# First head pair of an attention kernel: decays on 128 rows, a cumulative sum in two parts, identity products in PE's waits

## The chip, the cores and the metric

The kernel runs on one core of a Trainium2 chip. The metric is the device time of one execution in microseconds. A profiled execution lists for every instruction its engine, start and duration. The engines are PE (TensorE, the matrix engine; its weight loads are listed as PEld), DVE (VectorE), ACT (ScalarE), POOL (GpSimd) and SP (SyncE, which here only issues DMAs). Each takes its instructions in the order in which they stand in its queue.

## The reference

Attention with a forget gate, and two mixtures of experts behind it. Only the attention matters here:

```
scores = scale * np.matmul(q, k.transpose(0, 1, 3, 2))
log_f = np.log(np.clip(f, 0.0001, 1.0))
cum = np.cumsum(log_f, axis=-1)
decay = cum[:, :, :, None] - cum[:, :, None, :]
scores = np.where(causal, -1000000000.0, scores + decay)
scores = scores - np.max(scores, axis=-1, keepdims=True)
attn = np.exp(scores)
attn = attn / (np.sum(attn, axis=-1, keepdims=True) + 1e-09)
return np.matmul(attn, v).astype(np.float32)
...
x = _moe_ref(x=x, **moe_kwargs)
return _moe2_ref(x=x, **moe2_kwargs)
```

There are 2 batches of 8 heads, 576 positions and a head dimension of 64. A row's softmax does not change when a constant is added to the row, so only the column term of `decay`, minus `cum` of the key's position, is needed.

## The kernel before, in words

The attention works on eight pairs of heads (`B * NP`), one pair after the other. A pair has five steps: four blocks of 128 query rows (i = 0 to 3), each with the keys up to its diagonal, and a tail (i = 4) of the last 64 rows of both heads together. The loop at the end of the attention runs over all 40 steps `n`; in one turn it transposes the exponentials of step n - 2 (`emit_tp`), makes the scores of step n (`emit_s`) and, one turn later still, multiplies the transposed exponentials with v (`emit_av`). Steps 0 and 1 of pair 0 are made by `startup` ahead of the loop. The schedule is manual: each engine's queue has the order in which the code is written.

Scores need more precision than one pass of the matrix engine in its fast float type (F32R) gives. So k is split in a high part `kh` (a cast by DVE) and a low part `kl` (a subtraction by POOL). One tile `qa` holds the high part of q in one half of its rows and the low part in the other (a cast, then `q_low`, a subtraction on 64 rows by POOL or DVE). For every head a score block is three products that add up in one bank: `qa` with `kh` (L315), `qa` with `kl` (L316) and an identity with the causal mask (L317). DVE then adds the decay `bi` and takes the row's extreme in one instruction (an eviction, L323), ACT takes the exponential (L326). The key split of a pair is `split_k` (cast L290, subtractions L293), the q split `split_q` (cast L301, subtractions by the helper `sub`, L156).

For pairs 1 to 7 the decays come by DMA from `nbd`, a copy of minus eight times the cumulative sum in memory, spread to 128 partitions. Pair 0 cannot wait for that. It makes its decays on PE: `neg8[:, h:h + 1]` broadcast over 128 columns as the weights, 16 rows deep, times `cum` (L542), and ACT copies them to `bi` (L544). The cumulative sum itself is one scan on 16 partitions by DVE over 576 columns (L506), behind a clip (L503) and a logarithm by ACT (L504, with its table load). ACT loads the exponential's table ahead of the first exponential (L326).

While PE waits for the cumulative sum it does seven products of the identity with itself, 128 columns each (L510, `WARM`). They go to a bank that nobody reads. An ordinary float product is carried out as two passes, each with its own weight load, so seven products are 14 in the profile.

SP issues in this order: `f`, pair 0's k and q in two parts, pair 1's k and q, v of pair 0, two small tables (`dps`, `wgs`), `nbd`, pair 0's tail decays, then pair 2's k and q, pair 1's decays and v.

Of the kernel before, what the change touches and what calls it, by code (L numbers as in the profile page):

```python
# [40 lines left out]
NX = 5  # L41
LAG_TP, LAG_AV = 2, 3
AVS = {1: (0, 1), 3: (2, 3), 4: (4,)}
WARM = 7


@with_exitstack
def kernel(
# [180 lines left out]
    with ExitStack() as at:  # L229
# [9 lines left out]
        ps_a = pool(at, "ps_a", 1, space=PSUM)  # L239

        identb, neg8, maskd, maskt = [sm_p.tile(sh, dt, name=nm, bufs=1) for nm, sh, dt in (
            ("identb", [P, P], BF16), ("neg8", [B * H, B * H], F32), ("maskd", [P, P], BF16), ("maskt", [P, 64], BF16))]
        kls = [spl_p.tile([P, 2, S], F32R, tag=f"kl{i}", name=f"kl_{i}", bufs=1) for i in range(2)]
        state = {}

        def load_qk(p):
            raw = raw_p.tile([P, QKW], F32, tag="raw", name=f"qk_{p}")
            SY.dma_start(out=raw[:, QW:QKW], in_=qk[p, :, QW:QKW])
            SY.dma_start(out=raw[:, 0:QW], in_=qk[p, :, 0:QW])
            state[p] = dict(raw=raw)  # L250
# [51 lines left out]
            for h in range(2 if p > 1 else 1):  # L302
                q_low(p, h, G)

        def emit_s(p, i, between=lambda: None):
            st = state[p]
            qa, kh, kl, bi = st["qa"], st["kh"], st["kl"], st["bi"]
            if i < 4:
# [3 lines left out]
                for h in range(2):  # L312
                    ps = ps_s.tile([P, 512], F32, tag="ps", name=f"s_{p}_{i}_{h}")
                    q0 = TOPAD * h + i * P
                    T.matmul(out=ps[:, :n], lhsT=qa[:, q0:q0 + P], rhs=kh[:, h, :n], start=True, stop=False)  # L315
                    T.matmul(out=ps[:, :n], lhsT=qa[:, q0:q0 + P], rhs=kl[:, h, :n], start=False, stop=False)  # L316
                    T.matmul(out=ps[:, i * P:w], lhsT=identb, rhs=maskd, start=False, stop=True)  # L317
# [161 lines left out]
        def startup():  # L479
            ft = e_p.tile([B * H, S], F32, tag="e0", name="ft")  # L480
            SY.dma_start(out=ft, in_=f)
            first_loads()
            bi = bia_p.tile([P, 3, S], F32, tag="bias", name="bias_0")
            vt = raw_p.tile([P, 5, P], F32, tag="v", name="v_0")
            G.memset(neg8, 0.0)
# [5 lines left out]
            G.memset(ident, 0.0)  # L491
            G.affine_select(out=ident, in_=ident, compare_op=ALU.not_equal, fill=1.0, base=0,
                            pattern=[[-1, P]], channel_multiplier=1)
            one_s = e_p.tile([B * H, S], F32, tag="e0", name="one_s")
            V.memset(one_s, 1.0)
            for h in range(2):
                V.memset(kls[0][64 - 64 * h:128 - 64 * h, h, :].bitcast(F32), 0.0)
# [24 lines left out]
            def k_part(c0, c1):  # L522
                V.tensor_copy(out=kh[:, :, c0:c1], in_=rk[:, :, c0:c1])
                for h in range(2):
                    rows = slice(64 * h, 64 * h + 64)
                    G.tensor_tensor(out=kl[rows, h, c0:c1], in0=rk[rows, h, c0:c1],
                                    in1=kh[rows, h, c0:c1].bitcast(F32), op=ALU.subtract)

            def q_part(c0, c1):
                if c0 == 0:  # L530
                    A.copy(out=sq[:, :, c0:c1], in_=rq[:, :, c0:c1])
                else:
                    V.tensor_copy(out=sq[:, :, c0:c1], in_=rq[:, :, c0:c1])
                for h in range(2):
                    rows = slice(64 - 64 * h, 128 - 64 * h)
                    V.tensor_tensor(out=sq[rows, h, c0:c1], in0=rq[rows, h, c0:c1],
                                      in1=sq[rows, h, c0:c1].bitcast(F32), op=ALU.subtract)

            def bias_part(c0, c1):
                for h in range(2):  # L540
                    ps = ps_a.tile([P, 512], F32, tag=("rp", "avt")[h], name=f"b_{c0}_{h}")
                    T.matmul(out=ps[:, 0:c1 - c0], lhsT=neg8[:, h:h + 1].to_broadcast([B * H, P]),  # L542
                             rhs=cum[:, c0:c1], start=True, stop=True)
                    A.copy(out=bi[:, h, c0:c1], in_=ps[:, 0:c1 - c0])  # L544

            load_qk(1)
            SY.dma_start(out=vt, in_=v[0])
            SY.dma_start(out=dps, in_=dp)
            SY.dma_start(out=wgs, in_=wg)
            k_part(0, CUT)  # L550
            q_part(0, CUT)
            bias_part(0, P)
            emit_s(0, 0)
            k_part(CUT, S)
            bias_part(P, 2 * P)
            nb8 = e_p.tile([B * H, S], F32, tag="e0", name="nb8")
            V.tensor_scalar(out=nb8, in0=cum, scalar1=-8.0, scalar2=None, op0=ALU.mult)
# [4 lines left out]
            emit_s(0, 1)  # L562
            q_part(CUT, TOPAD)
            for h in range(2):
                G.memset(kls[1][64 - 64 * h:128 - 64 * h, h, :].bitcast(F32), 0.0)
            bias_part(2 * P, S)

        def patterns():
            G.memset(upper, 1.0)
# [21 lines left out]

        steps = [(p, i) for p in range(B * NP) for i in range(5)]
        at.enter_context(tc.manual_schedule())
        startup()
        for n in range(2, len(steps) + LAG_AV):
            if n == len(steps) + 1:
                early_product("p1")
            if 0 <= n - LAG_TP < len(steps):
                emit_tp(*steps[n - LAG_TP])
                if steps[n - LAG_TP][1] == 3:  # L600
                    emit_inv(steps[n - LAG_TP][0])
            if n == len(steps) + 1:
# [12 lines left out]
            if n < len(steps):  # L615
                p, i = steps[n]
                nx = p + 1 if p + 1 < B * NP else None
                if (p, i) == (0, 2):
                    split_k(1)
                    split_q(1)  # L620
                    patterns()
                if p and i == 1 and nx:
                    split_q(nx)
                if i == 4 and p + 2 < B * NP:
                    split_k(p + 2)
                if i == (1 if p else 3) and nx:
                    if p + 2 < B * NP:
                        load_qk(p + 2)
                    load_pair(nx)
# [789 lines left out]
```

## Time and profile before

| | us |
|---|---|
| median of 3 runs | 604.86 (603.96 to 605.48) |
| the profiled execution, its own time | 604.12 |
| its span, first to last instruction | 602.4 |
| PE busy | 589.4 (98%) |
| DVE, ACT, POOL busy | 322.7, 262.2, 331.2 |

A busy share is a mean over stages. The first 36 us are read here instruction by instruction; PE's busy time counts an instruction from its start to the end of its drain, so neighbours overlap. The time from one start to the next is PE's pace. Pair 0 runs from 0 to about 22.6 us, pair 1 from there to 35.28.

### The profile page before, as it was taken

What the parts mean: (1) busy time and instruction counts of PE and PEld (TensorE: products, weight loads), DVE (VectorE), ACT (ScalarE), POOL (GpSimd) and SP (SyncE); (2) the same over time, 40 slices, a digit from 0 to 9 for tenths busy, and PEclk for the clock granted to TensorE, in tenths of its full rate; (3) what the DMA queues carried; (4) which work ended last, traced back from release to release, by engine and by line L of the source; (5) the groups of instructions that cost most, each with busy time, mean ns of one, the idle gap of its engine ahead of it and who ended that gap; (6) DMA issues with size and microseconds to landing.
All of it is one profiled execution on the core that took longest, in us unless ns stands there. A gap on an engine that the chain in (4) does not pass through costs nothing. (4 is left out here: it accounts for less than half of the span.)

```text
span 602.4 us, 10714 instructions
## 1 busy us (share of the span) xinstructions
PE 589.4 (98%) x3981; PEld 491.9 (82%) x3981; DVE 322.7 (54%) x821; ACT 262.2 (44%) x665; POOL 331.2 (55%) x382
## 2 busy tenths in 40 slices
PE   8999999999999999999999999999999999999995
PEld 6788888998898898998998989989989775555674
DVE  6888877655454544544544535535436467311483
ACT  5678798674243343334334325315314222112481
POOL 4878989799278169159239329419614143322321
PEclk9999999999999999999999999999999999999999
DMA  6895730401112011011101201102255976999940
GB/s 210 265 319 166 264 108 23 140 27 55 63 70 71 1 67 40 35 26 48 67 1 70 71 1 70 71 1 71 70 210 226 357 277 223 411 419 423 382 156 24
DMA packets 19175, 84.32 MB, mean 140 GB/s; under 512 B 2965, under 2 KB 4001, under 8 KB 11953
## 3 DMA queue, kind: packets, MB, share of 16 engines
q1 hardware_dynamic: 16832, 73.19, 33.7%
q0 software_dynamic: 2288, 10.42, 4.4%
q8 instruction: 32, 0.52, 0.4%
q14 instruction: 23, 0.18, 0.1%
HBM read 79.57 MB, written 5.28 MB: 141 GB/s over the span
## 5 line engine op out<-in xcount | busy, mean ns | idle before, releaser
L872 PE MATMUL dn<-w2h,hh 128*128 128x512 f32 x288 | 114.4, 397 | 0.0
L874 PE MATMUL dn<-w2h,hl 128*128 128x512 f32 x288 | 112.4, 390 | 0.0
L873 PE MATMUL dn<-w2l,hh 128*128 128x512 f32 x288 | 112.2, 390 | 0.0
L884 DVE SCALAR_TENSOR_TENSOR acc<-dn,dps,acc 128x512 f32<-128x512 f32 (+1 forms) x64 | 47.4, 743 | 97.9 <-PE dn L874 97.7
L156 POOL TENSOR_TENSOR w2l<-rawd,w2h 128x512 fp32r<-128x512 f32 x32 | 40.5, 1296 | 94.5 <-ACT w2h L201 94.5
L220 PE MATMUL p<-xb_h,w 128*128 128x320 f32 x224 | 69.2, 309 | 0.0
L219 PE MATMUL p<-xb_l,w 128*128 128x320 f32 x224 | 69.2, 309 | 0.0
L218 PE MATMUL p<-xb_h,w 128*128 128x320 f32 x224 | 69.1, 309 | 0.0
L874 PEld LDWEIGHTS dn<-w2h,hl 128*128 128x128 f32 x288 | 54.0, 188 | 11.5
L872 PEld LDWEIGHTS dn<-w2h,hh 128*128 128x128 f32 x288 | 54.1, 188 | 11.3 <-issue 1.4
L873 PEld LDWEIGHTS dn<-w2l,hh 128*128 128x128 f32 x288 | 54.1, 188 | 9.9
L218 PE MATMUL p<-xa,w 128*128 128x256 f32 x218 | 61.3, 281 | 0.0
L220 PE MATMUL p<-xa,w 128*128 128x256 f32 x218 | 61.2, 281 | 0.0
L219 PE MATMUL p<-xa,w 128*128 128x256 f32 x218 | 61.2, 281 | 0.0
L201 ACT CAST w2h<-rawd 128x512 fp32r<-128x512 f32 x32 | 18.3, 621 | 84.8 <-PE dn L874 84.8
L156 POOL TENSOR_TENSOR hl<-m,hh 128x256 fp32r<-128x256 f32 (+1 forms) x32 | 25.8, 808 | 43.4 <-ACT hh L834 43.4
L828 DVE SCALAR_TENSOR_TENSOR hl<-p,hh 128x320 fp32r<-128x320 f32 (+1 forms) x62 | 28.5, 459 | 36.0 <-ACT hh L827 36.0
L156 POOL TENSOR_TENSOR w<-ws,w 128x512 fp32r<-128x512 f32 x32 | 40.7, 1297 | 3.4 <-ACT w L175 3.4
L219 PEld LDWEIGHTS p<-xb_l,w 128*128 128x128 f32 x224 | 42.0, 188 | 0.3
L218 PEld LDWEIGHTS p<-xb_h,w 128*128 128x128 f32 x224 | 42.1, 188 | 0.3
L220 PEld LDWEIGHTS p<-xb_h,w 128*128 128x128 f32 x224 | 42.1, 188 | 0.0
L218 PEld LDWEIGHTS p<-xa,w 128*128 128x128 f32 x218 | 41.3, 190 | 0.3
(292 smaller groups left out, 1333.8 us busy)
## 6 DMA issues: line engine op xcount, KB each, us to landing
wm<-in_m SPq DMA_DIRECT2D x32, 1024.0 KB, 10.1
rawu<-in_w SPq DMA_DIRECT2D x8, 1024.0 KB
rawd<-in_w SPq DMA_DIRECT2D x8, 1024.0 KB, 4.7
qk<-in_qk SPq DMA_DIRECT2D x7, 640.0 KB
qk<-in_qk SPq DMA_DIRECT2D x7, 576.0 KB
bias<-nbd SPq DMA_DIRECT2D x14, 288.0 KB, 6.9
v<-in_v SPq DMA_DIRECT2D x8, 320.0 KB, 5.3
bias<-nbd SPq DMA_DIRECT2D x16, 144.0 KB, 6.2
```

The source lines that it names most:

```text
L156: eng.tensor_tensor(out=out, in0=a, in1=b, op=ALU.subtract)
L201: A.copy(out=ws["d", u][0][:, c, :], in_=wr["d", u][:, c, :])
L218: T.matmul(out=ps, lhsT=wt[:, 0, a, i, :], rhs=xh[:, i, :], start=(i == 0), stop=False)
L219: T.matmul(out=ps, lhsT=wt[:, 0, a, i, :], rhs=xl[:, i, :], start=False, stop=False)
L220: T.matmul(out=ps, lhsT=wt[:, 1, a, i, :], rhs=xh[:, i, :], start=False, stop=(i == 1))
L828: V.scalar_tensor_tensor(out=hl[:, j, cs], in0=c, scalar=0.0, in1=hh[:, j, cs].bitcast(F32), op0=ALU.max, op1=ALU.subtract)
L872: T.matmul(out=ps, lhsT=hh[:, j, ks], rhs=wh[:, j, :], start=(j == 0), stop=False)
L873: T.matmul(out=ps, lhsT=hh[:, j, ks], rhs=wl[:, j, :], start=False, stop=False)
L874: T.matmul(out=ps, lhsT=hl[:, j, ks], rhs=wh[:, j, :], start=False, stop=(j == 3))
L884: V.scalar_tensor_tensor(out=a, in0=ps[:, c0:c1], scalar=pe, in1=a, op0=ALU.mult, op1=ALU.add)
```

## The change

Decay products. `neg8` and `cum` now have 128 rows. Rows 16 to 127 of both are zero there (a clear of `cum` on DVE, a wider `neg8` on POOL), and the product takes all 128 rows. The two halves of a decay (`bias_mm` on PE, `bias_copy` on ACT) are written apart, and the first two share a bank.

Cumulative sum. The scan is made over the first 256 columns, and later over the other 320 from the first one's last column on; the clear and the first decay of 128 columns stand between. `nb8` and the store to `nbd` come ahead of the first eviction.

Identity products. `fill(n)` puts n products of the identity with its first 64 columns into PE's queue, to a bank that nobody reads. There are 18, 3, 2, 5, 2 and 5 of them (`FILLS`) at six places, the last in the loop's first turn. The identity is the first thing that POOL makes.

Order of work. In the first two score blocks of pair 0 the products with `kl` come behind those with `kh` and the mask of both heads (`gaps`). The subtractions of q are cut in smaller pieces over DVE and POOL. The clears of `kl` all go to POOL. The exponential's table is loaded by a small exponential (`junk`) ahead of the bias copies. Pair 1's key split moves from behind step 2 to the end of `startup`, pair 2's from behind step 4 of pair 0 to behind step 0 of pair 1. SP issues pair 1's decays and v ahead of pair 2's k and q, and the two small tables last.

PE's queue at the start of the program, before: the decay products are `b_...`, the score blocks of pair 0 `s_<block>_<head>`, the transposes `tp_<block>_<head>`.

```order
L510 MATMUL warm<-ident 128x128 x7
L542 MATMUL b_0_207<-cum,neg_143 128x128
L542 MATMUL b_1_210<-cum,neg_143 128x128
L315 MATMUL s_0_0_213<-kh_192,qa_191 128x256
L316 MATMUL s_0_0_213<-kl_146,qa_191 128x256
L317 LDWEIGHTS identb
L317 MATMUL s_0_0_213<-maskd,identb 128x128
L315 MATMUL s_0_1_217<-kh_192,qa_191 128x256
L316 MATMUL s_0_1_217<-kl_146,qa_191 128x256
```

The same place now (`hot` is the bank of the identity products):

```order
L524 MATMUL hot_189<-ident 128x64 x18
L550 MATMUL b_0_213<-cum,neg_143 128x128
L550 MATMUL b_1_215<-cum,neg_143 128x128
L524 MATMUL hot_189<-ident 128x64 x3
L315 MATMUL s_0_0_236<-kh_191,qa_190 128x256
L318 LDWEIGHTS identb
L318 MATMUL s_0_0_236<-maskd,identb 128x128
L315 MATMUL s_0_1_239<-kh_191,qa_190 128x256
L318 LDWEIGHTS identb
L318 MATMUL s_0_1_239<-maskd,identb 128x128
L323 MATMUL s_0_0_236<-kl_146,qa_190 128x256
L550 MATMUL b_0_213<-cum,neg_143 128x128
```

More identity products stand ahead of the first decays, and three between these and the first scores; the product with `kl` has gone behind the second head's.

DVE's queue where pair 0 ends and pair 1 starts, before (`sn_t` are the evictions of pair 0's tail, `kh_399` is the key cast of pair 2, `qa_301` the low part of q of pair 1):

```order
L344 ISA sn_t,mn_t_388<-s_t_382,bias_157,mn_t_380 128x288
L344 ISA mn_t_388 128x1
L290 CAST kh_399<-qk_352 128x1152
L156 TENSOR_TENSOR qa_301<-qk_195,qa_301 64x640
L377 COPY et_3_1_418<-tp_3_1_413 128x512
L355 SCALAR_TENSOR_TENSOR rs_194<-sum_193 128x9
```

The same place now (`qa_306` is that low part, `kh_468` the key cast of pair 2):

```order
L349 ISA sn_t,mn_t_420<-s_t_414,bias_160,mn_t_412 128x288
L349 ISA mn_t_420 128x1
L156 TENSOR_TENSOR qa_306<-qk_157,qa_306 64x640
L382 COPY et_3_1_443<-tp_3_1_438 128x512
L360 SCALAR_TENSOR_TENSOR rs_193<-sum_192 128x9
L361 RECIPROCAL sum_192<-rs_193 128x9
L328 ISA sn_0_0_457,mn_0_0_458<-s_0_0_449,bias_271 128x128
L328 ISA mn_0_0_458 128x1
L328 ISA sn_0_1_462,mn_0_1_463<-s_0_1_453,bias_271 128x128
L328 ISA mn_0_1_463 128x1
L290 CAST kh_468<-qk_389 128x1152
```

The key cast of pair 2 has gone from ahead of pair 1's low part of q to behind the first two evictions of pair 1.

The diff, cut to its core:

```diff
-WARM = 7
+FILLS = (18, 3, 2, 5, 2, 5)
...
+                for h in range(2 if gaps else 0):
+                    gaps[h]()
+                    q0 = TOPAD * h + i * P
+                    T.matmul(out=pss[h][:, :n], lhsT=qa[:, q0:q0 + P], rhs=kl[:, h, :n], start=False, stop=True)
...
-            cum = e_p.tile([B * H, S], F32, tag="sneg", name="cum")
-            V.tensor_tensor_scan(out=cum, data0=one_s, data1=lf, initial=0.0, op0=ALU.mult, op1=ALU.add)
-
-            warm = ps_s.tile([P, 512], F32, tag="ps", name="warm")
-            for j in range(WARM):
-                T.matmul(out=warm[:, 0:P], lhsT=ident, rhs=ident, start=True, stop=True)
+            def scan(c0, c1):
+                V.tensor_tensor_scan(out=cum[0:B * H, c0:c1], data0=one_s[:, c0:c1], data1=lf[:, c0:c1],
+                                     initial=cum[0:B * H, c0 - 1:c0] if c0 else 0.0, op0=ALU.mult, op1=ALU.add)
+
+            hot = ps_a.tile([P, 512], F32, tag="avm", name="hot_0")
+
+            def fill(n):
+                for j in range(n):
+                    T.matmul(out=hot[:, 0:64], lhsT=ident, rhs=ident[:, 0:64], start=True, stop=True)
...
+            def bias_mm(c0, c1, o):
+                for h in range(2):
+                    if o == 0:
+                        bps[h] = ps_a.tile([P, 512], F32, tag=("rp", "avt")[h], name=f"b_{c0}_{h}")
+                    T.matmul(out=bps[h][:, o:o + c1 - c0], lhsT=neg8[:, h:h + 1].to_broadcast([P, P]),
+                             rhs=cum[:, c0:c1], start=True, stop=True)
...
+            fill(FILLS[0])
+            scan(0, CUT)
+            bias_mm(0, P, 0)
+            fill(FILLS[1])
+            V.tensor_copy(out=kh[:, :, 0:CUT], in_=rk[:, :, 0:CUT])
+            A.copy(out=sq[:, :, 0:CUT], in_=rq[:, :, 0:CUT])
+            junk = sm_p.tile([P, 1], F32, tag="mn", name="junk")
+            A.activation(out=junk, in_=ident[:, 0:1], func=AF.Exp)
+            for h in range(2):
+                k_low(h, 0, CUT)
+                q_lo(h, 0, P, V)
+            for h in range(2):
+                q_lo(h, P, CUT, G)
+            scan(CUT, S)
...
+            bias_copy(0, P, 0)
+            emit_s(0, 0, gaps=(lambda: None, lambda: (bias_mm(P, CUT, P), fill(FILLS[2]))))
+            V.tensor_copy(out=kh[:, :, CUT:S], in_=rk[:, :, CUT:S])
+            V.tensor_copy(out=sq[:, :, CUT:TOPAD], in_=rq[:, :, CUT:TOPAD])
+            for h in range(2):
+                k_low(h, CUT, S)
+            bias_copy(P, CUT, P)
+            fill(FILLS[3])
...
+            load_pair(1)
+            emit_s(0, 1, gaps=(lambda: None, lambda: None))
+            q_lo(0, CUT, TOPAD, V)
+            q_lo(1, CUT, TOPAD, G)
+            bias_mm(CUT, S, 0)
+            bias_copy(CUT, S, 0)
+            fill(FILLS[4])
+            split_k(1)
...
                 emit_tp(*steps[n - LAG_TP])
+                if n == LAG_TP:
+                    fill(FILLS[5])
...
                 if (p, i) == (0, 2):
-                    split_k(1)
                     split_q(1)
...
-                if i == 4 and p + 2 < B * NP:
+                if p and i == 4 and p + 2 < B * NP:
                     split_k(p + 2)
+                if (p, i) == (1, 0):
+                    split_k(2)
```

## Rows read from the trace of the kernel before

**Rows 1.** The page's first table: busy us (share of the span) and instructions.

```profile
PE 589.4 (98%) x3981; PEld 491.9 (82%) x3981; DVE 322.7 (54%) x821; ACT 262.2 (44%) x665; POOL 331.2 (55%) x382
```

**Rows 2.** Timeline of PE, pair 0: start us, us, instruction, idle before and releaser.

```profile
2.27 3.35 PE L510 MATMUL warm<-ident 128*128 128x128 f32 x14 [2.27 <-POOL ident L492]
5.89 1.22 PE L542 MATMUL b<-cum,neg 16*128 16x128 f32 x4 [0.27 <-DVE cum L506]
...
11.43 2.50 PE L542 MATMUL b<-cum,neg 16*128 16x320 f32 x4
13.86 0.69 PE L372 MATMUL tp<-ident,e 128*128 128x128 f32 x2
14.20 0.67 PE L315 MATMUL s<-kh,qa 128*128 128x384 f32 x1
...
20.29 0.88 PE L414 MATMUL avm<-et,v 128*64 128x128 f32 x12
...
22.64 0.39 PE L315 MATMUL s<-kh,qa 128*128 128x256 f32 x1 [0.44 <-POOL qa L156]
...
23.98 0.39 PE L315 MATMUL s<-kh,qa 128*128 128x256 f32 x1 [0.77 <-DVE qa L156]
```

**Rows 3.** Stretches: each engine's busy us, then PEclk, DMA share and GB/s.

```profile
0.00:17.50 17.50, 14.96 (x52) 11.29 (x52) 11.21 (x30) 9.36 (x23) 6.38 (x16) 1.00 0.64 213
...
601.20:602.40 1.20, 0.00 (x0) 0.00 (x0) 0.00 (x0) 0.00 (x0) 0.00 (x0) 0.50 0.00 0
```

**Rows 4.** Timeline of PE, pair 1, to the first score of pair 2.

```profile
24.87 0.36 PE L315 MATMUL s<-kh,qa 128*128 128x256 f32 x1
...
25.23 0.36 PE L315 MATMUL s<-kh,qa 128*128 128x256 f32 x1
...
28.19 0.43 PE L315 MATMUL s<-kh,qa 128*128 128x384 f32 x1
...
29.27 0.95 PE L425 MATMUL avt<-et_t,v 128*64 128x64 f32 x20
...
33.63 0.88 PE L414 MATMUL avm<-et,v 128*64 128x128 f32 x12
...
35.28 0.37 PE L315 MATMUL s<-kh,qa 128*128 128x256 f32 x1
```

**Rows 5.** Float products: groups by line (busy us, mean ns), and one from the timeline.

```profile
L510 PE MATMUL warm<-ident 128*128 128x128 f32 x14 | 3.4, 432 | 2.3 <-POOL ident L492 2.3
L1048 PE MATMUL xtl<-sel,acc 128*128 128x64 f32 x8 | 1.1, 281 | 0.0
503.38 1.10 PE L1048 MATMUL xtl<-sel,acc 128*128 128x64 f32 x8
```

**Rows 6.** Timeline of the other engines, pair 0 and pair 1.

```profile
0.79 0.10 POOL L485 MEMSET neg<- 16x16 f32 x1 [0.29 <-POOLq L1409]
...
1.65 0.20 POOL L491 MEMSET ident<- 128x128 f32 x1
...
6.24 1.82 POOL L526 TENSOR_TENSOR kl<-qk,kh 64x256 fp32r<-64x256 f32 x2 [4.03 <-DVE kh L523]
...
7.43 1.28 ACT L326 ACT_TABLE_LOAD   x1
...
11.62 1.50 POOL L565 MEMSET kl<- 64x576 f32 x2
...
21.03 1.55 POOL L156 TENSOR_TENSOR qa<-qk,qa 64x640 fp32r<-64x640 f32 x1
...
21.30 1.90 DVE L290 CAST kh<-qk 128x1152 fp32r<-128x1152 f32 x1
...
23.12 0.81 DVE L156 TENSOR_TENSOR qa<-qk,qa 64x640 fp32r<-64x640 f32 x1
...
34.31 0.76 DVE L290 CAST kh<-qk 128x1152 fp32r<-128x1152 f32 x1
```

**Rows 7.** PE's waits from 26 to 130 us: us in total, times, longest.

```profile
PE s L315 <- DVE mn L323: 0.6, 2, 0.3
```

More of the change, by code (lines that the diff above doesn't have):

```diff
@@ L241 @@
         identb, neg8, maskd, maskt = [sm_p.tile(sh, dt, name=nm, bufs=1) for nm, sh, dt in (
-            ("identb", [P, P], BF16), ("neg8", [B * H, B * H], F32), ("maskd", [P, P], BF16), ("maskt", [P, 64], BF16))]
+            ("identb", [P, P], BF16), ("neg8", [P, B * H], F32), ("maskd", [P, P], BF16), ("maskt", [P, 64], BF16))]
         kls = [spl_p.tile([P, 2, S], F32R, tag=f"kl{i}", name=f"kl_{i}", bufs=1) for i in range(2)]
@@ L303, in split_q, with emit_s @@
                 q_low(p, h, G)
-        def emit_s(p, i, between=lambda: None):
+        def emit_s(p, i, between=lambda: None, gaps=None):
             st = state[p]
@@ L315, in emit_s @@
                     T.matmul(out=ps[:, :n], lhsT=qa[:, q0:q0 + P], rhs=kh[:, h, :n], start=True, stop=False)
-                    T.matmul(out=ps[:, :n], lhsT=qa[:, q0:q0 + P], rhs=kl[:, h, :n], start=False, stop=False)
-                    T.matmul(out=ps[:, i * P:w], lhsT=identb, rhs=maskd, start=False, stop=True)
+                    if not gaps:
+                        T.matmul(out=ps[:, :n], lhsT=qa[:, q0:q0 + P], rhs=kl[:, h, :n], start=False, stop=False)
+                    T.matmul(out=ps[:, i * P:w], lhsT=identb, rhs=maskd, start=False, stop=not gaps)
                     pss.append(ps)
+                for h in range(2 if gaps else 0):
+                    gaps[h]()
+                    q0 = TOPAD * h + i * P
+                    T.matmul(out=pss[h][:, :n], lhsT=qa[:, q0:q0 + P], rhs=kl[:, h, :n], start=False, stop=True)
                 between()
@@ L482, in startup @@
             first_loads()
+            load_qk(1)
             bi = bia_p.tile([P, 3, S], F32, tag="bias", name="bias_0")
             vt = raw_p.tile([P, 5, P], F32, tag="v", name="v_0")
+            SY.dma_start(out=vt, in_=v[0])
+            G.memset(ident, 0.0)
+            G.affine_select(out=ident, in_=ident, compare_op=ALU.not_equal, fill=1.0, base=0,
+                            pattern=[[-1, P]], channel_multiplier=1)
             G.memset(neg8, 0.0)
@@ L490, in startup @@
                             pattern=[[-1, P]], channel_multiplier=1)
-            G.memset(ident, 0.0)
-            G.affine_select(out=ident, in_=ident, compare_op=ALU.not_equal, fill=1.0, base=0,
-                            pattern=[[-1, P]], channel_multiplier=1)
+            for j in range(2):
+                for h in range(2):
+                    G.memset(kls[j][64 - 64 * h:128 - 64 * h, h, :].bitcast(F32), 0.0)
             one_s = e_p.tile([B * H, S], F32, tag="e0", name="one_s")
             V.memset(one_s, 1.0)
-            for h in range(2):
-                V.memset(kls[0][64 - 64 * h:128 - 64 * h, h, :].bitcast(F32), 0.0)
+            cum = e_p.tile([P, S], F32, tag="sneg", name="cum")
+            V.memset(cum, 0.0)
             V.tensor_copy(out=identb, in_=ident)
@@ L539, in bias_part @@
[L539 to L555, printed above, removed]
+            def k_low(h, c0, c1, eng=G):
+                rows = slice(64 * h, 64 * h + 64)
+                sub(eng, kl[rows, h, c0:c1], rk[rows, h, c0:c1], kh[rows, h, c0:c1].bitcast(F32))
+            def q_lo(h, c0, c1, eng):
+                rows = slice(64 - 64 * h, 128 - 64 * h)
+                sub(eng, sq[rows, h, c0:c1], rq[rows, h, c0:c1], sq[rows, h, c0:c1].bitcast(F32))
@@ new lines, in startup, with bias_copy @@
+            bps = {}
+            def bias_mm(c0, c1, o):
+                for h in range(2):
+                    if o == 0:
+                        bps[h] = ps_a.tile([P, 512], F32, tag=("rp", "avt")[h], name=f"b_{c0}_{h}")
+                    T.matmul(out=bps[h][:, o:o + c1 - c0], lhsT=neg8[:, h:h + 1].to_broadcast([P, P]),
+                             rhs=cum[:, c0:c1], start=True, stop=True)
+            def bias_copy(c0, c1, o):
+                for h in range(2):
+                    A.copy(out=bi[:, h, c0:c1], in_=bps[h][:, o:o + c1 - c0])
@@ L556, in startup @@
+            scan(CUT, S)
             nb8 = e_p.tile([B * H, S], F32, tag="e0", name="nb8")
-            V.tensor_scalar(out=nb8, in0=cum, scalar1=-8.0, scalar2=None, op0=ALU.mult)
+            V.tensor_scalar(out=nb8, in0=cum[0:B * H], scalar1=-8.0, scalar2=None, op0=ALU.mult)
             SY.dma_start(out=nbd, in_=nb8)
+            bias_copy(0, P, 0)
+            emit_s(0, 0, gaps=(lambda: None, lambda: (bias_mm(P, CUT, P), fill(FILLS[2]))))
+            V.tensor_copy(out=kh[:, :, CUT:S], in_=rk[:, :, CUT:S])
@@ L561, in startup @@
                 SY.dma_start(out=bi[rows, 2, :], in_=nbd[h:h + 1, :].partition_broadcast(64))
[L562 to L566, printed above, removed]
+            load_pair(1)
[6 more added lines that the diff above has]
+            split_k(1)
+            return fill
         def patterns():
@@ L593 @@
         at.enter_context(tc.manual_schedule())
-        startup()
+        fill = startup()
         for n in range(2, len(steps) + LAG_AV):
@@ L628 @@
                         load_qk(p + 2)
-                    load_pair(nx)
+                    if p:
+                        load_pair(nx)
+                    else:
+                        SY.dma_start(out=dps, in_=dp)
+                        SY.dma_start(out=wgs, in_=wg)
                 if (p, i) == (0, 4):
```

13 lines of the change are left out of this document (removed).

## The prediction

> **What bounds the kernel now.** I read the page's first table first: PE is busy for 98% of the span [rows 1], and no other engine for more than about half of it. A change in the first head pair is therefore worth what it takes out of PE's path up to where PE runs without gaps. So I next read PE's timeline of the first 36 us, and the list of PE's waits behind it: from 26 to 130 us the largest group is 0.6 us in all [rows 7]. The measuring point is the first score product of the second head of pair 1. It starts at 23.98 us [rows 2]; what makes it earlier should make the end earlier by as much.
>
> Up to there three things cost PE time. First, the clock. A 384-column score product takes 0.67 us at 14.20 [rows 2] and 0.43 us in pair 1 [rows 4]. The table of stretches shows a granted clock of 1.00 for the first 17.5 us [rows 3]; of the stretches I asked for only the last, after the work, has 0.50, so the column says nothing of the start, and the durations must be read instead. At about 17.5 us the timeline's shapes change from the one pace to the other: to there TensorE is at 1.2 GHz, from there at 2.4. Ahead of the rise PE did this: identity products from 2.27 to 5.62, decay products on 16 rows, scores with waits, decay products on 16 rows again until 13.86, then 3.6 us of transposes and scores without a gap [rows 2]. Second, the order: PE's first scores stand behind casts and subtractions of three engines. Third, two stalls ahead of pair 1, 0.44 us for POOL's low part of q and 0.77 us for VectorE's [rows 2]. The latter is late because the cast of pair 2's keys stands in front of it and takes 1.90 us instead of 0.76 [rows 6].
>
> **The change, part by part.**
> *Products with the identity.* The seven of 128 columns go, 35 of 64 columns come (18+3+2+5+2+5), and all stand in PE's queue ahead of needed work. Price at 1.2 GHz: the old ones took 3.35 us for 14 passes [rows 2]; less the last pass (0.43) that is 2.92/13 = 0.225 a pass, 0.45 a product [rows 5]. For 64 columns the nearest row is a group of 64-column float products near the end: 1.10 us for eight passes, less the last of 0.28, is 0.117 a pass, so 0.235 a product at 2.4 GHz [rows 5], and twice that, 0.47, at 1.2. So half the columns are no cheaper; each pass has a weight load of 128 columns, and that seems to set the pace. I take 0.45 and 0.235. The other end is half of it, 0.225 and 0.12, if only the streamed columns counted.
> The Trainium skill (TensorE: Matmul & The Clock Gate, "LDWEIGHTS (loading the stationary operand)") puts a load at its columns over 1.2 GHz, 107 ns for 128; by it a product of two loads would cost 0.21 at either clock, and the first 18 would take 3.9 us. The rows agree near 2.4 GHz (0.117 a pass) and not at 1.2, where a pass of the old products has 0.225.
>
> *When the clock rises.* The identity is now made first on POOL. From its first step at 1.65 to PE's start at 2.27 it took 0.62 us, and POOL's first step comes at 0.79 [rows 2, 6], so PE starts at about 1.4 and has no gap from there. Nearest row: the gapless run from 13.86 had the full clock after 3.6 us, so 5.0 us is the early end. But the run 2.27 to 5.62 did not bring it, so I allow a late end of 8.2 and take 6.5, about the middle. That these products raise the clock at all no row shows (rival A).
>
> *PE's path with the rise at 6.5.* First 18 products: 5.1/0.45 = 11.3 before the rise, 6.7 x 0.235 = 1.6 behind: end at 8.1. Two decay products: 0.85 us at 1.2 GHz (1.22 with the drain of the last [rows 2]), 0.43 at 2.4: 8.5. The cumulative sum is no limit: over all 576 columns it let PE go at 5.89 [rows 2], and 256 columns of it end sooner. Three products 0.7: 9.2. First scores at 0.36 a head (24.87 to 25.23 [rows 4]) 0.72, with two decays 0.43 and two products 0.47 between: 10.8. Five products 1.2: 12.0. Second scores 0.72: 12.7. The decays of 320 columns took 11.43 to 13.86, 2.43 [rows 2]; half: 13.9. Two products 0.47, two transposes 0.17 (half of 13.86 to 14.20 [rows 2]), five products 1.2: 15.8. That is 1.6 later than 14.20. From there PE's order is that of pair 1 from 28.19 to 35.28, 7.1 us, without the tail products of 0.95 [rows 4]: 6.2. Pair 1 starts at 22.0, its second head at 22.4.
>
> *The stalls.* VectorE's low part of q must be ready by 22.4. Pair 2's key cast no longer stands ahead of it, so it follows the last eviction of pair 0. Before, VectorE was free of that at 21.30 [rows 6], 1.0 behind the start of the attention-times-v products at 20.29 [rows 2]. These now start at 15.8 + (33.63 - 28.19) - 0.95 = 20.3 [rows 4]; 1.0 and the subtraction's 0.81 [rows 6] give 22.1. POOL's half depends on pair 1's casts, which move up to the second and third steps. Both fit, with little room.
>
> *At nothing.* The exponential's table load, 1.28 us, moves ahead of the first bias copies, which were done when it began at 7.43 [rows 6]; at worst they come at 8.7, and PE's decays, which they read, now end at 8.5. The four clears of the low parts go to POOL, 0.75 us each, from about 2.2 to 5.2; behind them the first key subtractions, 1.82 us [rows 6], are done at 7.1, again ahead of PE. If PE were earlier, these two would be the next waits (rival B). Cumulative sum and decays on 128 rows: PE's columns are the same. DMA: the loads for pair 1 leave SyncE earlier and ahead of pair 2's, the two small tables later; pair 1's first need of them is at 22.
>
> *Sum.* 23.98 - 22.4 = 1.6 us. The profiled execution took 604.12 us (span 602.4 and 1.7 around it), so 602.5. The median before is 604.86, 0.7 more; against it this is 2.4 us, 0.4%. With the rise at 5.0 the first 18 end 0.8 earlier (601.7), at 8.2 0.9 later (603.4).
>
> **Rivals.**
> *A, slower: the products do not bring the clock.* Place: PE's queue ahead of the first decays. All runs at 1.2 GHz: 18 x 0.45 = 8.1, to 9.5; decays 0.85, three products 1.35: 11.7; scores 1.44, decays 0.85, two products 0.9: 14.9; five products 2.25, scores 1.44, decays 2.43: 21.0; two products, transposes, five products 3.5: third scores at 24.5, 10.3 late. From there as before, less the stalls of 1.2: 9.1 late, 613. It decides from a rise at about 9.7 on, since each us of delay costs half a us; a rise at 12 to 15 gives 605 to 607. For it: the old products, 3.35 us without a gap, brought nothing. Against: these run on for longer, and go over into decays and scores without a gap, as the run from 13.86 did.
> *B, much faster: a product costs its columns only.* 18 x 0.225 = 4.1, to 5.5; decays 6.3; then at 2.4 GHz third scores at about 11.6, 4.2 earlier than above. I put 1 us of it down as lost to VectorE, which has two casts, six evictions and three copies between there and the tail: 599.3. The 0.117 a pass stands against it.
> *C, no difference: the gain turns into waits of VectorE and POOL for each other.* The cast that took 1.90 instead of 0.76 began at 21.30, inside a POOL subtraction that ran from 21.03 to 22.58, and ended at 23.20 [rows 6]: 0.62 behind it, nearly its whole 0.76. After the change pair 1's key cast stands by POOL's low part of q in the same way, and pair 2's between pair 1's evictions: 1.14 us if one of them reaches PE. That gives 603.6.
> The Trainium skill (SBUF — State Buffer, "SBUF: two separate sides") says that whichever of VectorE and GpSimd starts first holds the shared port for the whole instruction; the 1.90 agrees, and by it this rival is real at both new places. Against: the path above leaves either cast over a us before PE needs what follows.
>
> **How the numbers follow.** From no change this kernel can tell about 0.3%, 1.8 us: faster is under 603.0, slower over 606.7. My forecast has 0.55 (602.5, own range 601.4 to 603.6), A 0.14 and a late rise 0.11, B 0.08, C 0.12. Faster: 0.47 of the forecast, all of B, 0.02 of C: 0.57. Same: 0.08 of the forecast, 0.10 of C, 0.04 of the late rises: 0.22. Slower: A and 0.07 of the late rises: 0.21. The range of 599 to 607.5 leaves out A and half of B, 0.18.
>
> **What would show it.** Right: products of 0.45, then 0.235 us; the change of pace between 5 and 8.2 us; the third scores of pair 0 between 15 and 16.7; pair 1's second head at 22 to 23 with no wait of over 0.3 us ahead of it. Wrong: products of 0.225 at the start (B), a pace that changes only behind 10 us (A), key casts of over 1.5 us with PE waiting on VectorE (C), or a PE that waits in pair 1 or 2 where before it had none.

## The result, and the profile after

The changed kernel takes 610.39 us (median of 6 runs, 608.66 to 610.62), the kernel before 604.41 beside it (6 runs, 603.51 to 605.97): ratio 1.0089, 95% interval 1.0069 to 1.0109. It is slower by 6.0 us; I had forecast faster by 2.4. Its profiled execution took 608.66 us with a span of 607.0, 4.6 more than before.

The first table of its page is close to that of [rows 1], with 7.2 us more of PE:

```profile
PE 596.6 (98%) x4037; PEld 500.7 (82%) x4037; DVE 322.8 (53%) x820; ACT 261.8 (43%) x666; POOL 334.2 (55%) x387
```

The timeline of PE of the changed kernel, pair 0 up to the measuring point, answers to [rows 2] (start us, us, instruction, idle time before it and its releaser; `hot` are the products with the identity, `b` the decays, `s` the scores):

```profile
1.42 7.94 PE L524 MATMUL hot<-ident 128*128 128x64 f32 x36 [1.42 <-POOL neg L495]
9.15 1.17 PE L550 MATMUL b<-cum,neg 128*128 128x128 f32 x4
10.11 1.38 PE L524 MATMUL hot<-ident 128*128 128x64 f32 x6
11.25 0.56 PE L315 MATMUL s<-kh,qa 128*128 128x256 f32 x1
...
14.44 2.23 PE L524 MATMUL hot<-ident 128*128 128x64 f32 x10
16.43 0.56 PE L315 MATMUL s<-kh,qa 128*128 128x256 f32 x1
...
17.90 2.34 PE L550 MATMUL b<-cum,neg 128*128 128x320 f32 x4
20.03 0.66 PE L524 MATMUL hot<-ident 128*128 128x64 f32 x4
...
20.75 1.23 PE L524 MATMUL hot<-ident 128*128 128x64 f32 x10
21.79 0.42 PE L315 MATMUL s<-kh,qa 128*128 128x384 f32 x1
...
28.73 0.36 PE L315 MATMUL s<-kh,qa 128*128 128x256 f32 x1
```

Read the same shape at two places. Ten passes of the products take 2.23 us at 14.44 and 1.23 at 20.75; a 256-column score takes 0.56 at 16.43 and 0.36 at 28.73. The pace changes at 20.0 to 20.2 us (the trace's record of the granted clock has the rise to 2.4 GHz at 20.24; for the kernel before it has it at 17.50). So the first 18 products, 7.7 us without a gap, did not bring the 2.4 GHz, and everything up to the 320-column decays ran at 1.2. Pair 0's third scores start at 21.79 instead of 14.20, pair 1's second head at 28.73 instead of 23.98: 4.75 later, and the span is 4.6 longer.

Behind that place nothing is new. PE's waits from 26 to 130 us, for [rows 7]:

```profile
PE s L315 <- DVE mn L328: 0.6, 2, 0.3
```

The stalls of 0.44 and 0.77 us ahead of pair 1 [rows 2] are gone, as forecast. VectorE's casts of the next two pairs' keys take 0.76 us at both their new places; that of pair 2, the second here, had taken 1.90 [rows 6]:

```profile
19.42 0.76 DVE L290 CAST kh<-qk 128x1152 fp32r<-128x1152 f32 x1
...
30.34 0.76 DVE L290 CAST kh<-qk 128x1152 fp32r<-128x1152 f32 x1
```

### The profile page after: what moved, and what is told of

It is laid out like the page before. It is cut to its first block, busy times and chain, and to the rows that moved or that the text cites. A ratio compares the mean times of both kernels' runs of the same rounds, so it can differ in the third digit from the quotient of the medians.

```text
span 607.0 us, 10836 instructions
## 1 busy us (share of the span) xinstructions
PE 596.6 (98%) x4037; PEld 500.7 (82%) x4037; DVE 322.8 (53%) x820; ACT 261.8 (43%) x666; POOL 334.2 (55%) x387
## 5 line engine op out<-in xcount | busy, mean ns | idle before, releaser
L331 ACT ACTIVATE e<-sn,mn 128x128 f32<-128x128 f32 (+3 forms) x64 | 35.5, 555 | 14.9 <-DVE mn L328 12.6
```

The costliest lines, as they stand in the source:

```text
L331: A.activation(out=e[:, :w], in_=sneg[:, :w], func=AF.Exp, bias=mn, scale=-1.0, accum_out=st["sum"][:, 2 * i + h:2 * i + h + 1])
```

## The experiments

Theories. **N (narrow products):** a product of 64 columns behind weight loads of 128 does not bring the clock, it only stands in front of needed work. **T (time):** gapless work brings it after some time, whatever its shape, and something else kept it down. **R (rows):** decays on 128 rows bring the clock sooner than on 16. **D (order):** the stalls came from the order of the casts.

All places are those of the profiled execution of each run; "rise" is the record's first step to 2.4 GHz, "second head" the first score of pair 1's second head. The rises of two executions can lie 3 us apart for the same work: the same fourteen wide products from 1.42 on brought it at 7.45 in e9's and at 4.45 in e12's. Times are medians; the kernel before had 603.52 to 603.93 us beside them.

| run | rise | second head | time (runs) | ratio to before, interval |
|---|---|---|---|---|
| before | 17.50 | 23.98 | 604.41 (6) | |
| changed | 20.24 | 28.73 | 610.39 (6) | 1.0089 (1.0069 to 1.0109) |
| e1 products 128 wide | 4.91 | 21.51 | 603.52 (12) | 0.9991 (0.9981 to 1.0000) |
| e11 loads 64 wide | 5.83 | 20.73 | 603.97 (10) | 0.9997 (0.9984 to 1.0011) |
| e2 no products | 9.66 | 21.04 | 602.37 (6) | 0.9968 (0.9957 to 0.9980) |
| e5 first 18 alone | 12.53 | 23.75 | 605.77 (9) | 1.0043 (1.0028 to 1.0058) |
| e6 later 17 alone | 18.78 | 26.66 | 608.02 (4) | 1.0078 (1.0059 to 1.0097) |
| e7 none, 16 rows | 18.94 | 23.13 | 604.21 (11) | 1.0008 (0.9999 to 1.0017) |
| e3 before, 128 rows | 11.82 | 23.00 | 602.67 (12) | 0.9977 (0.9968 to 0.9986) |
| e4 before, cast moved | 17.01 | 23.32 | 602.63 (6) | 0.9976 (0.9962 to 0.9990) |
| e8 before, ten products | 6.62, 16.86 | 22.88 | 602.48 (12) | 0.9991 (0.9979 to 1.0003) |
| e9 fourteen wide | 7.45 | 20.70 | 602.93 (12) | 0.9985 (0.9972 to 0.9998) |
| e12 e9, q on VectorE | 4.45 | 20.49 | 603.67 (12) | 1.0003 (0.9985 to 1.0021) |
| e10 before, three edits | 7.71 | 21.33 | 601.83 (6) | 0.9961 (0.9947 to 0.9976) |

### What the products do

```diff
# e1: the changed kernel, each product 128 columns wide
-   T.matmul(out=hot[:, 0:64], lhsT=ident, rhs=ident[:, 0:64], ...)
+   T.matmul(out=hot[:, 0:P], lhsT=ident, rhs=ident, ...)
```

> The changed kernel with the identity products 128 columns wide instead of 64, in the same number and places. Theory 1: the 64-column products did not bring the higher clock (the pace changed at 20.2 us, behind a run of scores and decays), and 128-column products, gapless from 1.4 us, do. Then the pace changes between 5 and 8.2 us inside the first 18, the third scores of pair 0 start at 15 to 16.7 us, pair 1's second head at 22 to 23, time 601.5 to 603.5 (the path that I forecast for the change). Theory 2: identity products do not bring it at either width; then the pace changes at 17 to 24 us as in the changed kernel, and the time is 608.5 to 611, since a pass of 128 columns takes the 0.225 us that one of 64 does.

```profile
1.42 5.94 PE L524 MATMUL hot<-ident 128*128 128x128 f32 x36 [1.42 <-POOL neg L495]
7.19 0.61 PE L550 MATMUL b<-cum,neg 128*128 128x128 f32 x4
...
14.55 0.43 PE L315 MATMUL s<-kh,qa 128*128 128x384 f32 x1
...
21.51 0.36 PE L315 MATMUL s<-kh,qa 128*128 128x256 f32 x1
```

PE's timeline again: twice the columns, yet the 36 passes end sooner than in the changed kernel, since the pace changes inside them, at 4.9 us. The decays take 0.61 instead of 1.17. Width alone moves pair 1 by 7.2 us and the ratio from 1.0089 to 0.9991. T falls, since these products take no more time than those that brought nothing. N stands. Rise, third scores and second head came a little earlier than I expected (4.91, 14.55 and 21.51 for 5 to 8.2, 15 to 16.7 and 22 to 23), and the time still lies at the upper end of its range.

```diff
# e11: the changed kernel, each product half in its weights too
+   T.matmul(out=hot[0:64, 0:64], lhsT=ident[:, 0:64], rhs=ident[:, 0:64], ...)
```

> The changed kernel with its 35 products cut to half in their weights too: 64 columns of the identity loaded, 64 streamed, into 64 rows of the result. Theory 1 (the weight load sets the pace of a pass, as I took it): a pass at the slow pace takes 0.11 to 0.15 us in place of 0.22, the first 18 end at 5.4 to 6.9; if then the share of time in which columns stream is what counts, the clock rises inside them or behind them by 8 us, and the time falls to 602 to 604.5. If it is the width of the product that counts, the rise comes as late as behind 9.15 us, 13 to 19, and the time is 604 to 607 for the shorter products alone. Theory 2 (a fixed cost sets the pace): a pass stays at 0.20 to 0.22, the first 18 end at 9.2, time 608 to 611 as the changed kernel's.

```profile
1.42 4.10 PE L524 MATMUL hot<-ident 128*64 128x64 f32 x36 [1.42 <-POOL neg L495]
6.50 0.68 PE L550 MATMUL b<-cum,neg 128*128 128x128 f32 x4 [0.97 <-DVE cum L517]
...
20.73 0.36 PE L315 MATMUL s<-kh,qa 128*128 128x256 f32 x1
```

The same 64 columns are streamed, behind half the load (and into half the rows of the result): 4.10/36 = 0.114 us a pass instead of 7.94/36 = 0.22. The rise comes at 5.83, behind the products' end at 5.52 and ahead of the first decay at 6.50, so nothing but the products can have brought it. So the weight load did set the pace, as theory 1 has it, and 64 columns as such are not too few: they left the clock down only behind loads of twice their width. Pair 1 is 8.0 us earlier than in the changed kernel by this edit alone. The spread of 3 us does not blur this: the six traced executions with ten or more wide products, or with half loads, have their rise by 7.71 (e1, e8 to e12), the three with narrow products behind full loads at 12.53 or later (changed, e5, e6).

```diff
# e2: the changed kernel without products; e5: the first 18 alone; e6: the other 17 alone
- FILLS = (18, 3, 2, 5, 2, 5)
+ FILLS = (0, 0, 0, 0, 0, 0)     # e2
+ FILLS = (18, 0, 0, 0, 0, 0)    # e5
+ FILLS = (0, 3, 2, 5, 2, 5)     # e6
```

> The changed kernel without any identity product. Theory 1 (the products themselves, at the low clock in PE's queue, are the loss): the first decays start at about 6.4 us, when the first part of the cumulative sum is there (9.15 with the products), the third scores of pair 0 at 14 to 14.5 (21.8 with), the clock rises between 13.5 and 17.5, pair 1's second head at 20.5 to 22, time 600.5 to 602.5. Theory 3 (the loss lies in the other engines' new order, above all the clears on POOL that slow VectorE's first steps by 1 us): the third scores stay behind 17 us with PE waiting for VectorE or POOL, and the time at 605 to 608.

> The changed kernel with its first 18 products of 64 columns alone; the 17 later ones are left out. Theory (narrow products do not bring the clock, they only stand ahead of the decays): the first decay product starts at about 9.15 us as in the changed kernel, PE keeps the slow pace through it, and the rise follows the first decay by about what it did without any product (9.66 - 6.49 = 3.2 us), at 12 to 13. Pair 1's second head, 21.04 without any product, comes up to 2.7 later, less the 1.44 us that it then waited for POOL: 22.3 to 23.7; time 603.6 to 605.1. Rival (products of 64 columns hold the clock down for what follows too): rise at 17 us or later, second head past 25, time over 606.5.

> The changed kernel without its first 18 products, with the 17 later ones (3, 2, 5, 2, 5) of 64 columns. Theory 1 (the later ones are what keeps the pace slow: they fill PE between the decays and scores with work of few columns): the rise comes late, at 14 to 18 us, pair 1's second head at 24.5 to 26.5, time 606 to 608. Theory 2 (they cost only their own time, and the scores bring the rise as without any product): rise at 10 to 12, the later products mostly 0.235 us each, second head at 22 to 24, time 603.5 to 605.

PE's timeline without any product:

```profile
6.49 1.19 PE L550 MATMUL b<-cum,neg 128*128 128x128 f32 x4 [6.49 <-DVE cum L517]
...
9.67 0.28 PE L315 MATMUL s<-kh,qa 128*128 128x256 f32 x1
...
14.68 0.44 PE L315 MATMUL s<-kh,qa 128*128 128x384 f32 x1 [1.44 <-POOL qa L156]
...
21.04 0.36 PE L315 MATMUL s<-kh,qa 128*128 128x256 f32 x1
```

PE does nothing for 6.5 us, and the clock still rises at 9.66, 10.6 us before the changed kernel's: decays on 128 rows and scores bring it. The second head in e5, and then in e6:

```profile
23.75 0.36 PE L315 MATMUL s<-kh,qa 128*128 128x256 f32 x1
```

```profile
26.66 0.36 PE L315 MATMUL s<-kh,qa 128*128 128x256 f32 x1
```

Neither group is free. The first 18 are 7.7 us long, of which PE would have waited all but 2.7; at pair 1 they cost 23.75 - 21.04 = 2.7 us (the first decay starts 2.7 later, and the rise 2.9). The later 17 are 5.7 us long in e6's timeline and cost 26.66 - 21.04 = 5.6 us: they stand between the decays and scores that brought the rise in e2, and it comes only at 18.78; against that, PE no longer waits the 1.44 us for POOL. Together 8.3; the changed kernel has 7.7. For e6 that is theory 1, at or just past the upper end in rise, place and time; for e5 the first theory, with the rise where it was expected (12 to 13), the place at the upper end and the time 0.7 us above it.

### What the decays' rows do

```diff
# e7: the changed kernel without products, decays on 16 rows;  e3: the kernel before, decays on 128 rows
-   T.matmul(..., lhsT=neg8[:, h:h + 1].to_broadcast([P, P]), rhs=cum[:, c0:c1], ...)
+   T.matmul(..., lhsT=neg8[:, h:h + 1].to_broadcast([B * H, P]), rhs=cum[0:B * H, c0:c1], ...)
# e8: the kernel before
- WARM = 7
+ WARM = 10
```

> The changed kernel without any identity products and with the decays on 16 rows, as before the change; the order is the changed one. Theory 1 (the rows bring the rise forward, as they did in the old order from 17.50 to 11.82 us): the rise comes later than 9.66, at 12 to 15 us, pair 1's second head 1 to 2.5 later than 21.04, time 603.2 to 604.8. Theory 2 (in this order the scores alone bring it): rise at 9.5 to 10.5, second head at 21.0 to 21.4, time 602.1 to 602.7.

> The kernel before with one part of the change, the decays on 128 rows (zeros in rows 16 to 127). Theory 4 (decays on 16 rows kept the clock low from 11.4 to 13.9 us): the pace changes at about 14 us instead of 17.5, pair 1's second head at 23.3 instead of 24.0 (there it waits for VectorE's cast, so little of the gain gets through), time 603.5 to 604. Rival: rows make no difference, pace changes at 17 to 18 us, time as before within 0.1%.

> The kernel before with ten products of the 128-column identity in place of seven; nothing else. Theory 1 (products of 128 columns bring the rise once they run on for a little longer: beside the changed kernel they did it 3.5 us behind their start at 1.42): from 2.27 the rise comes at 5.7 to 6.0 us, the ten products end at 6.3 to 6.9 (before: seven at 5.62), the decays at 6.4 to 7.0 run fast. The third scores of pair 0 start at 12 to 13.3 instead of 14.20; pair 1's second head at 22 to 23.3 instead of 23.98, with the waits for POOL and VectorE ahead of it as large as before or larger; time 0.7 to 2 less than before, some 602.0 to 603.2. Theory 2 (it was the 128-row decays and scores behind the products that brought the rise, or the earlier start): rise at 15 us or later, the second head at 24 to 25, time 604 to 605.

PE's timeline of e7, and then the stretches of e8 (busy us of PE, PEld, DVE, ACT, POOL, then PEclk, DMA share, GB/s) and its timeline of PE:

```profile
12.02 2.50 PE L550 MATMUL b<-cum,neg 16*128 16x320 f32 x4
...
23.13 0.36 PE L315 MATMUL s<-kh,qa 128*128 128x256 f32 x1
```

```profile
6.60:10.00 3.40, 3.40 (x22) 2.54 (x21) 2.20 (x8) 2.69 (x8) 1.90 (x3) 1.00 1.02 398
10.00:16.80 6.80, 6.71 (x22) 4.04 (x20) 5.66 (x14) 4.06 (x14) 3.01 (x5) 0.50 0.48 133
```

```profile
2.27 4.56 PE L510 MATMUL warm<-ident 128*128 128x128 f32 x20 [2.27 <-POOL ident L492]
...
8.50 0.70 PE L542 MATMUL b<-cum,neg 16*128 16x128 f32 x4
...
10.16 2.50 PE L542 MATMUL b<-cum,neg 16*128 16x320 f32 x4
```

In the new order 16 rows put the rise off from 9.66 to 18.94 and pair 1 by 2.1 us, more on the clock than I expected (12 to 15), and 1.8 us in the median. In the old order 128 rows bring it forward from 17.50 to 11.82, though I had 14, and the time is 602.67, below the 603.5 to 604 that I had. Pair 1 comes 0.98 us earlier, although the clear of the new rows on VectorE puts the first decays off from 5.89 to 6.50. I had costed this edit at nothing.

Ten products of the full identity in the old kernel bring the rise at 6.62; seven, to 5.62, had not in the execution shown [rows 2]. But with 16-row decays it doesn't last: from 10.04 to 16.86 the granted clock is 0.50, and the 320-column decays take their old 2.50 us though they started 1.27 earlier. PE was busy for 6.71 of those 6.80 us. Neither of the two theories had a rise that falls back; pair 1 comes 1.1 us earlier, as the first had it, and the time is not told from no change.

### The order, and what is best

```diff
# e4: the kernel before, pair 2's key cast behind pair 1's first step
-                 if i == 4 and p + 2 < B * NP:
+                 if p and i == 4 and p + 2 < B * NP:
                      split_k(p + 2)
+                 if (p, i) == (1, 0):
+                     split_k(2)
```

> The kernel before with one part of the change, pair 2's key split moved from behind the last step of pair 0 to behind the first step of pair 1. Theory 5: the wait of 0.77 us for VectorE ahead of pair 1's second head goes, and the cast takes 0.76 to 1.0 us at its new place: time 603.5 to 603.8, 0.6 to 0.9 less. Rival (the cast delays pair 1's evictions there): a new wait of PE for VectorE in pair 1, no gain.

The 0.77 us for VectorE are gone and the second head starts 0.66 earlier, at 23.32, as D has it. The median is 1.3 below that of before, more than this place explains, and below the expected range. Part of it lies in the mix of executions: three of e4's six have a mean granted clock of 0.991 and took 601.9 to 602.6 us, the others 0.997 and 602.7 to 604.2. The kernel before took 602.5 to 602.9 at 0.991 (seven of the 27 executions beside e5 to e8, none of the 25 beside e4) and 603.4 to 603.8 at 0.996 to 0.998. e8's trace, with the rise that falls back, has 0.991 too; whether the kernel before has such early rises in some executions, no trace shows.

```diff
# e9: the changed kernel, fourteen products of 128 columns, none later
+ FILLS = (14, 0, 0, 0, 0, 0)    # and 128 columns as in e1
# e12: e9, and
- q_lo(1, CUT, TOPAD, G)
+ q_lo(1, CUT, TOPAD, V)
# e10: the kernel before with e3, e4 and e8 together
```

> The changed kernel with fourteen products of 128 columns at the start (in place of 18 of 64) and without the 17 later ones. Theory 1 (wide products bring the rise, 128-row decays keep it, and nothing stands in PE's way behind): rise at 4.9 us as with 18 wide ones, the products end at 6.3 to 6.6, the first decay starts at 6.5 to 6.7 at the fast pace (no product: 6.49 at the slow one). From there PE is ahead of the others, and the subtractions on POOL set the second head of the third step (14.68 without products): 14.2 to 14.7; pair 1's second head at 20.2 to 20.9, so only 0.1 to 0.8 before that without any product (21.04); time 0.3 to 0.8 less than its 602.4, some 601.5 to 602.4. Theory 2 (PE's waits behind the decays let the clock fall back, as in the kernel before with ten products): the record shows a fall between 8 and 12 us, second head at 21 to 22.5, time 602.3 to 603.5.

> As the fourteen wide products (and no later ones), with the low part of q's second head for the columns from 256 on moved from POOL to VectorE. Theory (POOL's subtractions set the second head of the third step): with one subtraction of 1.39 us less in POOL's queue, that head starts at 12.9 to 13.6 instead of 14.2 to 14.7, POOL's part of pair 1's q comes a good us earlier, pair 1's second head at 19.2 to 20.0; PE's end 0.5 to 1.2 earlier than with fourteen wide products alone, time 600.3 to 601.5. Rival (the scores wait for VectorE instead, which has 0.56 more): second head at 20.2 to 21, no difference in time.

> The kernel before with three edits together: ten products of the 128-column identity, decays on 128 rows, pair 2's key cast behind pair 1's first step. Theory 1 (the fall back of the clock at 10.04 us with ten products alone came from the decays on 16 rows): the rise at 6.6 now stays, the 320-column decays take about 1.3 us instead of 2.50, third scores of pair 0 at 12.5 to 13.6, pair 1's second head at 20.5 to 21.5 with no wait for VectorE; time 1.5 to 2.5 below the kernel before. Theory 2 (the fall came from PE's waits between the scores): the clock falls back again at 9 to 11 us, second head at 21.6 to 22.6, time 0.8 to 1.6 below the kernel before.

The three edits of e10 give the lowest median of this study, 601.83 us, ahead of before by 0.39% (0.24 to 0.53); e2's 0.32% (0.20 to 0.43) is not told from it. The rise stays, and decays, second head and time are as its first theory had them. The stretches of e10 show that 128 rows hold what ten products bring (its record has 2.4 GHz from 7.71 to 499), and PE's timeline the decays of 320 columns and pair 1:

```profile
6.60:10.00 3.40, 3.19 (x20) 2.70 (x20) 2.40 (x9) 2.44 (x6) 1.75 (x2) 1.00 1.01 367
10.00:16.80 6.80, 5.35 (x29) 3.33 (x29) 6.48 (x18) 4.04 (x16) 4.45 (x5) 1.00 0.47 143
```

```profile
10.47 1.34 PE L543 MATMUL b<-cum,neg 128*128 128x320 f32 x4
...
20.65 0.39 PE L315 MATMUL s<-kh,qa 128*128 128x256 f32 x1 [0.44 <-POOL qa L156]
...
21.33 0.38 PE L315 MATMUL s<-kh,qa 128*128 128x256 f32 x1
```

PE was less busy in that stretch than in e8's, 5.35 against 6.71 us, and kept the clock, so the fall in e8 was not from waits (theory 1). e9 and e12 reach pair 1 earlier still, and end later; in the new order no kernel with products has a lower median than the one without (e2). In e9 the rise came 2.5 us late and the decays with it, at 7.51, but the clock held through PE's waits, against its second theory. The second head is where it was expected (20.70): VectorE and POOL set it by then, not PE. Its time is 0.5 above the expectation. In e12 the third step's first head waits 0.62 us for VectorE, as in e9 (0.63), and its second head starts at 13.72, not at the expected 12.9 to 13.6 (e9: 13.89). Pair 1's second head gains only 0.2, as the rival had it, and PE later waits 1.0 us for VectorE where e9 does not.

### Where an earlier pair 1 goes

e1 is 2.47 us ahead of before at pair 1, 1.2 in its span. A ruler between is the first selection product behind the long mixture (`xsel`); with it the second transposition of the gathered rows (`tpx`). PE's timeline of before, of e1 and of e2, and of e2 the stretch around (columns as above):

```profile
500.77 1.52 PE L1005 MATMUL xsel<-acc,sel 128*64 128x256 f32 x12
...
512.25 0.42 PE L1129 MATMUL tpx<-ident,rows 128*128 128x128 f32 x2
```

```profile
498.33 1.51 PE L1039 MATMUL xsel<-acc,sel 128*64 128x256 f32 x12
...
511.86 0.44 PE L1163 MATMUL tpx<-ident,rows 128*128 128x128 f32 x2 [2.04 <-DMA rows<-out,idx]
```

```profile
497.87 2.83 PE L1039 MATMUL xsel<-acc,sel 128*64 128x256 f32 x12
```

```profile
497.00:504.00 7.00, 6.92 (x47) 4.38 (x48) 3.51 (x23) 0.85 (x8) 0.43 (x2) 0.76 0.92 337
```

Up to `xsel` the lead is whole: 2.44 us in e1, 2.90 in e2 (and the changed kernel's 505.60 is 4.83 late). Then e1 waits 2.04 us for gathered rows (its gathers landed 7.8 us behind their issue in the median, before 6.2), and e2's `xsel` runs at 1.2 GHz (the record has that from 497.77 to 501.18, the whole of it, so the stretch has 0.76). e11 (1.9 us) and e9 (1.8, though its gathers landed after 6.7) have the first kind, and e9's clock falls a little later, at 512.63; the profiled executions of e3, e5, e6, e7, e10 and e12 have the second. This is read from traces; no run took either away, so why PE has to wait or a clock falls there stays open. For these kernels `xsel` is the better measure of an edit in the first pairs; the ends differ by 1 to 2 us for reasons that these runs do not separate.

## Why the prediction was wrong

*The measuring point and what follows it* held: 4.75 us at pair 1, 4.83 at `xsel`, 4.6 in the span. PE's start at 1.42 was 1.4 in the sum.

*The price of a product* held: 7.94/18 = 0.44 us at 1.2 GHz against the 0.45 taken, and at the fast pace the five at 20.75 reach the next row after 1.04, 0.21 each against 0.235. Rival B is out. The Trainium skill (TensorE: Matmul & The Clock Gate, "LDWEIGHTS (loading the stationary operand)") gives a load one price, its columns over 1.2 GHz, with no word of the clock; that is 0.107 us for 128 columns. The trace agrees at 2.4 GHz (1.04/10 = 0.104 us a pass) and not at 1.2 (0.22).

*When the clock rises* is the step that failed. I took 6.5 us "about the middle" between 5.0, from the gapless run at 13.86, and 8.2; it was 20.24. I had read "without a gap" as what brings it. But in the price of the product I had already worked out that half the columns cost the same time, because the load sets the pace: so a pass is filled by the load and not by the stream, while the trace shows PE as busy throughout. That fact was in the sum for the price and not for the clock. e1 and e11 change nothing but the products' shape, and either brings the rise before 6 us. Why passes filled by the load leave the clock down, beyond these two edits, no run shows. Nor was the row "2.27 to 5.62 did not bring it" a sign against wide products: with three more it came (e8).

*PE's path* therefore ran as rival A worked it out, within 1 us, up to the 320-column decays: first scores at 11.25 (A: 11.7), five products at 14.44 (14.9), end of the decays at 20.03 (21.0). There the rise came, which A, all at 1.2 GHz, did not have, so the third scores start at 21.79 and not at 24.5, and the time is 608.7 to 610.6 and not 613. A late rise stood in the prediction, at 12 to 15 us for 605 to 607; it was later still. By the prediction's own half a us for each us of delay, a rise at 20.24 in place of 6.5 gives 602.5 + 6.9 = 609.4 against the 608.66 of the profiled execution: the one term explains the miss.

*Rows of the decays, "at nothing"*, was wrong the other way: they are worth 0.98 us at pair 1 in the old order and 2.1 in the new one (e3, e7). With no products the change would have been right by its sign, and 602.37 beside the forecast's 602.5, by another road.

*The stalls* went as predicted, 6.94 us from third scores to second head (forecast 6.6), and rival C's price appeared at neither place. That was luck: pair 1's cast, at 19.42, found POOL idle (from 18.68 to 20.26). Where PE was earlier it did not: the same cast takes 1.44 us in e1 and 1.45 in e9, where it starts at 13.01 inside a subtraction of POOL that runs from 12.63 to 13.83. The cast alone is worth 0.66 us there (e4).

*The clears on POOL, "at nothing"*, were hidden here by the 18 products. Without them the first decays wait for the cumulative sum until 6.49, where before they started at 5.89 [rows 2], though only 256 columns are summed (below).

## What to carry to other kernels

A busy PE in the profile is not a PE that brings its clock: 64-column products behind full weight loads left it at 1.2 GHz here, and twice the columns or half the load brought it. Look too at the shapes of the needed work around them, since 16 rows in place of 128 put the rise off, or lost it again, for more than the products gave. And measure an early gain at a ruler behind it (`xsel` here) as well as at the end, where other things may give it back.

## What the runs showed that I had not expected

*A rise can be lost in busy work*: in e8 the clock fell from 2.4 to 1.2 GHz at 10.04 us behind 3.4 us of scores and 16-row decays without a gap, and rose again at 16.86.

*Rows count for the clock*: the same decays on 128 rows instead of 16 moved the rise by 5.7 us (e3) and 9.3 us (e7 to e2), at the same length (1.22 us for the first four passes in before and e3). From start to start 128 rows are even a little cheaper: the first score follows the first decay after 0.88 us in e3 (1.15 before), and after 0.84 in e2 (1.11 in e7).

*VectorE's short work takes longer beside POOL's clears.* In the changed kernel the four clears of the low parts lie over two short operations of VectorE (timelines of POOL and VectorE):

```profile
2.82 2.62 POOL L503 MEMSET kl<- 64x576 f32 x4
```

```profile
2.79 1.24 DVE L511 COPY maskt<-maskd 64x64 bf16<-64x64 bf16 x2 [0.59 <-POOL maskd L499]
4.07 0.85 DVE L513 TENSOR_SCALAR lf<-ft 16x576 f32<-16x576 f32 x1
...
5.67 0.68 DVE L517 TENSOR_TENSOR_SCAN cum<-one_s,lf 16x256 f32<-16x256 f32 x1 [0.75 <-ACT lf L514]
```

Before, with POOL idle there, the same two took 0.35 and 0.45 us (timeline of VectorE, before):

```profile
2.91 0.35 DVE L501 COPY maskt<-maskd 64x64 bf16<-64x64 bf16 x2
3.29 0.45 DVE L503 TENSOR_SCALAR lf<-ft 16x576 f32<-16x576 f32 x1
4.49 1.35 DVE L506 TENSOR_TENSOR_SCAN cum<-one_s,lf 16x576 f32<-16x576 f32 x1 [0.75 <-ACT lf L504]
```

So the sum of 256 columns ends at 6.35, later than that of all 576 before (4.49 + 1.35 = 5.84). That the clears are the cause is argued from the overlap; no run moved them back.

*The clock may also fall in the middle*, as in e2's trace. It is a guess that this is also why the changed kernel's runs differ: four of its six, not traced, have a mean granted clock of 0.994 to 0.995 and took 610.3 to 610.6 us, the two with 0.998 (the traced one, without such a fall) and 0.999 took 608.7 and 609.1.
